# Three quarters of an output weight loaded in mid-run, in unequal shares per DMA engine: one decode step of attention and an MLP

## The chip, the cores and the metric

The kernel runs on one core of one Trainium2 chip. The core has a matrix engine (PE, with its weight loads shown as PEld), a vector engine (DVE), a scalar engine (ACT), GpSimd (POOL) and a queue engine (SP). All of them share 16 DMA engines that bring data from memory (HBM) to the on-chip buffer of 128 partitions. The metric is the device time of one execution in microseconds (us); less is better.

## The reference

One token, model width 512. Attention has 32 heads of 128 with a cache of 4096 keys and values each; beside it stands an MLP of 1376 hidden units; a gate mixes the two.

```python
g = sigmoid((x * gate_w).sum(-1))
q = (x @ wq).reshape(1, 1, 32, 128)                 # wq: 512 x 4096
p = softmax(einsum(q, k_cache) * 128 ** -0.5)       # per head: 4096 scores
a = einsum(p, v_cache).reshape(1, 1, 4096) @ wo     # wo: 4096 x 512
h = relu(x @ w1 + b1) ** 2                          # w1: 512 x 1376
b = h @ w2 + b2                                     # w2: 1376 x 512
out = g * a + (1 - g) * b
```

Everything is bf16. The caches are 32 MB each, `wq` and `wo` 4 MB each, `w1` and `w2` 1.4 MB each: 78 MB are read once for an output of 1 KB.

## The kernel before, in words

**Order of the loads.** SP issues nearly all loads into one queue, in the order of the program: four pieces of `wq` into the buffer `W`, then K and V of each head by turns, K seven heads (`LAG`) ahead of V. Each K or V is 1 MB: 128 partitions, 8 KB in each, which the 16 DMA engines share evenly. Eight buffers each (`Kt`, `Vt`); a K buffer is loaded again once DVE (`s_sd`) and PE (`s_t`) have read it, a V buffer once PE has (`s_pv`). After V 8 come the four pieces of `w1`, after V 10 the whole of `w2` (`w2a` in one load with 10 KB in each partition, `w2b` for the last 96 rows).

**Work per head.** For half of the keys DVE multiplies and sums (`ttr`, L579); for the other half PE turns them (`transposes`, L385), ACT copies them out (`evac`, L319) and PE takes the product with q (`scores`, L396). Every four heads the maxima are joined (`max_rows`, `max_cols`), ACT takes the exponentials (`exps`, L330), PE sums over the values (`pv`, L421), and every eight heads DVE divides by the denominators and the gate (`norm`, giving eight columns of `onorm` and counting `s_on`). In iteration i of the PE's loop, `transposes(i)`, `scores(i-1)` and `pv(i-7)` follow each other.

**The output weight.** `W` is free for `wo` once all of `wq` was used (`s_qps` 8, in iteration 21). `wo` is used in two parts, each laid out so that a partition holds several neighbouring rows. The first `NA` = 16 heads are the first 64 such long rows of `woa_v` (32 rows of `wo`, 32 KB each), which go to partitions 32 to 95. GpSimd loads 60 of them, in four groups, each a load of 12 partitions and one of 3. The cursor that decides at which DMA engine a load starts is reset ahead of each group, and a dummy load of 4 partitions (`dm`) goes first. Head 3 (`HX`) is left out there and is loaded by SP at the end (`wox`). The other 16 heads follow from SP in three pieces of 8, 6 and 2 rows per partition (`TS`, L251), which overwrite `W`; so SP waits for PE's last use of the first part (`s_wa`).

Because `wo` lies in long rows, the attention output must be laid out likewise. For the first part: `turn_a` (PE) turns `onA`, DVE copies it to `oA`, `spread_a` (PE) spreads it with a matrix of zeros and ones (`selA`) to `o2A`, and `out_a` makes 128 small matmuls in four quarters (iterations 28 to 31) into `acc`. For the second part `regroup` does this at the end of the run with `selB`, and `out_b` makes the matmuls, a piece at a time as it lands. The matrices are built by GpSimd in place of `w1`, once that was used (`s_h`).

**The MLP.** `mlp_h` (PE, iteration 24) makes the hidden layer, DVE squares it, and `mlp_out` (iteration 27, L451) adds its product with `w2` to `acc`.

**The end.** Behind the last data SP issues fifteen tiny loads, of 1 to 15 partitions (L254), then waits for the result and stores it. DVE adds the bias to `acc` (L655), PE turns the sum (L541), DVE copies it (L657).

Of the kernel before, what the change touches and what calls it, by code (L numbers as in the profile page):

```python
# [5 lines left out]
def bass_gated_mix__gqa_block_cached__dense_activation_squared_relu__decode_kernel(  # L6
# [47 lines left out]
    NA = 16  # L54
    HX = 3
    A0 = 32
    TB = 16
    TS = [0, 8, 14, 16]
    NW = len(TS) - 1

# [4 lines left out]
    wob_v = A_wo[NA * 128:NH * 128, :].rearrange("(p t) n -> p t n", t=TB)  # L65
# [4 lines left out]
    with ctx:  # L70
# [14 lines left out]
        wox = W[:, TB * DM:TB * DM + DM]  # L85
# [3 lines left out]
        selB = w1_sb[0:NH - NA, 0, 0:1024].rearrange("h (c p) -> h c p", c=8)  # L89
        selA = w1_sb[0:NA, 1, 0:512].rearrange("h (c p) -> h c p", c=4)  # L90
# [8 lines left out]
        onA = sb("onA", [128, NA], bf16)  # L99
# [4 lines left out]
        dm = sb("dm", [4, 4, 2, 16], bf16)  # L104
        fin4 = sb("fin4", [4, 128], bf16)
        zeros = sb("zeros", [128, 128], bf16)
        xb = sb("xb", [128, 4, 128], bf16)
        ident = sb("ident", [128, 128], bf16)
# [29 lines left out]
        O2B = pS[:, 64:64 + TB]  # L138
# [3 lines left out]
        OTA = pQ[0:NA, 0:128]  # L142
        O2A = pQ[:, 128:160]
# [16 lines left out]
        s_w2 = sem("s_w2")  # L160
        s_wo = [sem(f"s_wo{t}") for t in range(NW)]
        s_wx = sem("s_wx")
        s_wp = [sem(f"s_wp{n}") for n in range(8)]
        s_dm = [sem(f"s_dm{n}") for n in range(4)]
        s_na = sem("s_na")
        s_at = sem("s_at")
        s_ac = sem("s_ac")
        s_wa = sem("s_wa")
# [50 lines left out]
        def _(eng):  # L219
# [16 lines left out]
            for h in range(NH):  # L236
# [8 lines left out]
                if h == 10:  # L245
                    eng.dma_start(w2a[:, :, :], w2_v).then_inc(s_w2, 16)
                    eng.dma_start(w2b[:, :], B_w2[FG * 128:F, :]).then_inc(s_w2, 16)
            eng.wait_ge(s_wa, 1)
            eng.dma_start(wox, A_wo[HX * 128:HX * 128 + 128, :]).then_inc(s_wx, 16)
            for c in range(NW):  # L250
                eng.dma_start(wo_sb[:, TS[c]:TS[c + 1], :], wob_v[:, TS[c]:TS[c + 1], :])\  # L251
                   .then_inc(s_wo[c], 16)
# [10 lines left out]
        def _(eng):  # L263
# [9 lines left out]
            HI = A0 + 4 * (HX + 1)  # L273
            LO = A0 + 4 * HX
            for r in range(4):
                eng.inc_swdge_sem([], [], mode="reset_dge_cursor")
                src = B_w1[0:4, 0:32].rearrange("p (a c) -> p a c", a=2)
# [5 lines left out]
            for q in s_dm:  # L283
                eng.wait_ge(q, 16)
# [60 lines left out]
        def _(eng):  # L345
# [122 lines left out]
            def out_a(n):  # L468
# [9 lines left out]
                if n == 3:  # L478
                    mm.then_inc(s_wa, 1)
# [16 lines left out]
            def out_b(c):  # L496
# [6 lines left out]
                if c == NW - 1:  # L503
                    mm.then_inc(s_acc, 1)
# [181 lines left out]
```

## Time and profile before

| | us |
|---|---|
| median of 3 runs | 198.80 (198.79 to 198.81) |
| the profiled execution | 198.97 |
| its span, first to last instruction | 197.1 |
| busy: PE / DVE / ACT / POOL | 132.0 / 129.2 / 79.5 / 11.7 |
| bytes moved by DMA | 78.75 MB, mean 400 GB/s |
| share of the chain that ended last: DMA / DVE / SP's queue / PE | 70% / 12% / 9% / 6% |
| GpSimd's loads: first issue, last landing | 106.2, 130.6 |
| last landing of V 31 / of the three last pieces of `wo` | 188.94 / 191.76, 193.63, 194.27 |

The page of the profile cuts the span into 40 equal slices and gives for each engine the busy tenths, the clock granted to PE, the mean busy share of the 16 DMA engines and what they moved. The stretches are the same with limits of one's own choice: for each engine the busy time and the number of instructions, then the clock, the DMA share and GB/s. The chain of waits is followed back from the last instruction, at each step to what released it. The records of the landings hold a time for each step of a load's semaphore; a load counts 1 for each DMA engine that has done its share.

### The profile page before, as it was taken

The numbers are of one execution on the slowest core, as the hardware profiler recorded it, in microseconds if no ns is written. First come the engines' busy times: TensorE is split into PE (matmuls) and PEld (weight loads), VectorE is DVE, ScalarE is ACT, GpSimd is POOL, SyncE is SP. The second block draws the span as 40 slices with busy tenths as digits, with TensorE's granted clock in tenths as the row PEclk, the third lists the DMA queues.
The fourth block names the chain that finished last, engine by engine and source line by source line (L and its number), as shares of the span: only waits on it lengthen the run. The fifth ranks groups of instructions, "written<-read, shape, count | busy, mean of one in ns | idle before, by whom it ended". The sixth has DMA issues, their size and how long they took to land.

```text
span 197.1 us, 6623 instructions
## 1 busy us (share of the span) xinstructions
PE 132.0 (67%) x2455; PEld 119.0 (60%) x2461; DVE 129.2 (66%) x1144; ACT 79.5 (40%) x148; POOL 11.7 (6%) x24
## 2 busy tenths in 40 slices
PE   0138657499886867915637476756999997994444
PEld 0105637478676667715635476756999987884443
DVE  0307999999998687716835677757759987760010
ACT  2105838466463436503306333633038432623000
POOL 2000000000000000000004900000070000000000
PEclk9999966755555555555558555555555555555555
DMA  6999999999999999999999999999999999999970
GB/s 221 427 427 424 421 421 422 412 421 421 416 417 421 416 422 403 420 424 385 414 421 416 419 416 411 408 426 417 421 417 417 421 412 419 417 421 421 412 296 21
DMA packets 12262, 78.75 MB, mean 400 GB/s; under 512 B 2035, under 2 KB 2261, under 8 KB 3030
## 3 DMA queue, kind: packets, MB, share of 16 engines
q1 hardware_dynamic: 11448, 76.36, 94.0%
q0 software_dynamic: 768, 1.97, 2.6%
q8 instruction: 19, 0.31, 0.6%
q14 instruction: 13, 0.11, 0.2%
q10 hardware_dynamic: 14, 0.01, 0.0%
HBM read 78.32 MB, written 0.00 MB: 397 GB/s over the span
## 4 chain that ended last, share of the span: by engine, by line
DMA 70%; DVE 12%; SPq 9%; PE 6%; issue 1%; ACT 0%
DMA Kt<-in_A_k_cache_dram 55%; DVE Kt L579 11%; DMA W<-in_A_wo_dram 9%; SPq L232 6%; DMA W<-in_A_wq_dram 6%; PE KP L385 2%; SPq L227 2%; PE pQ L363 1%; DVE S L579 1%; SPq L221 1%; PE pX L500 1%; PE pX L475 0%; PE pQ L421 0%; PE pX L421 0%; PE pS L396 0%
## 5 line engine op out<-in xcount | busy, mean ns | idle before, releaser
L579 DVE CUSTOM_DVE_ANT_0 Kt<-Kt,qb 128x128 bf16<-128x128 bf16 x512 | 111.2, 286 | 28.2 <-DMA Kt<-in_A_k_cache_dram 28.2
L319 ACT ACTIVATE kT<-KP 128x1024 bf16<-128x1024 bf16 x64 | 61.9, 1021 | 70.8 <-PE KP L385 70.8
L385 PE MATMUL KP<-ident,Kt 128*128 128x128 bf16 x512 | 56.6, 299 | 31.7 <-DMA Kt<-in_A_k_cache_dram 31.7
L385 PEld LDWEIGHTS KP<-ident,Kt 128*128 128x128 bf16 x512 | 49.1, 139 | 34.5 <-DMA Kt<-in_A_k_cache_dram 33.1
L579 DVE DVE_READ_ACCUMULATOR2_ANT S<- 128x1 f32 x512 | 41.7, 81 | 0.0
L396 PEld LDWEIGHTS pS<-qcol,kT 128*128 128x128 bf16 x512 | 19.0, 108 | 9.2 <-DVE S L585 9.2
L396 PE MATMUL pS<-qcol,kT 128*128 128x1 bf16 x512 | 19.2, 167 | 7.9 <-DVE S L585 7.9
L363 PE MATMUL pQ<-W,xb 128*128 128x512 bf16 x26 | 12.3, 614 | 7.7 <-DMA W<-in_A_wq_dram 6.3
L421 PEld LDWEIGHTS pO<-E,Vt 128*128 128x128 bf16 x512 | 15.6, 105 | 1.2 <-issue 0.8
L421 PE MATMUL pO<-E,Vt 128*128 128x1 bf16 x512 | 16.2, 166 | 0.0
L421 PE MATMUL pQ<-E,Vt 128*128 128x1 bf16 x256 | 8.1, 165 | 7.1 <-DMA Vt<-in_A_v_cache_dram 5.4
L421 PEld LDWEIGHTS pQ<-E,Vt 128*128 128x128 bf16 x256 | 7.6, 104 | 7.4 <-issue 6.0
L311 ACT ACTIVATE qb<-pQ 128x512 bf16<-128x512 f32 x8 | 4.7, 592 | 15.1 <-PE pQ L363 15.1
L363 PEld LDWEIGHTS pQ<-W,xb 128*128 128x128 bf16 x32 | 3.6, 130 | 10.7 <-issue 10.7
L330 ACT ACTIVATE E<-S,nM 128x32 bf16<-128x32 f32 x32 | 9.9, 310 | 0.3
L278 POOL DMA_DIRECT2D dm<-in_B_w_dram x4 | 2.6, 648 | 104.3 <-PE pQ L363 104.3
L421 PEld LDWEIGHTS pX<-E,Vt 128*128 128x128 bf16 x256 | 7.8, 104 | 0.7 <-issue 0.6
L421 PE MATMUL pX<-E,Vt 128*128 128x1 bf16 x256 | 8.1, 165 | 0.0
L600 DVE RECIPROCAL rden<-pM 128x8 f32<-128x8 f32 x4 | 0.8, 203 | 10.4 <-PE pM L427 10.4
L585 DVE COPY S<-pS 128x16 f32<-128x16 f32 x32 | 5.4, 169 | 2.7 <-PE pS L396 2.7
L565 DVE CAST qcol<-pQ 128x4 bf16<-128x4 f32 x8 | 1.2, 152 | 8.4 <-PE pQ L371 8.4
L588 DVE TENSOR_REDUCE mp<-S 128x1 f32<-128x32 f32 x32 | 6.0, 186 | 1.1
(84 smaller groups left out, 79.5 us busy)
## 6 DMA issues: line engine op xcount, KB each, us to landing
Kt<-in_A_k_cache_dram SPq DMA_DIRECT2D x32, 1024.0 KB, 26.9
Vt<-in_A_v_cache_dram SPq DMA_DIRECT2D x32, 1024.0 KB, 27.8
W<-in_A_wq_dram SPq DMA_DIRECT2D x4, 1024.0 KB, 7.8
W<-in_A_wo_dram POOLq DMA_DIRECT2D x4, 384.0 KB, 12.9
w_sb<-in_B_w_dram SPq DMA_DIRECT2D x4, 344.0 KB, 22.8
w2a<-in_B_w_dram SPq DMA_DIRECT2D x1, 1280.0 KB, 18.5
W<-in_A_wo_dram SPq DMA_DIRECT2D x1, 1024.0 KB, 16.7
W<-in_A_wo_dram SPq DMA_DIRECT2D x1, 768.0 KB, 18.1
```

The lines of the kernel that those rows point to most:

```text
L227: eng.dma_start(Kt[:, h % NK, :], k_h[h, :, :]).then_inc(s_k[h % NK], 16)
L232: eng.dma_start(Vt[:, h % NV, :], v_h[h, :, :]).then_inc(s_v[h % NV], 16)
L311: eng.activation(qb[:, c * 512:(c + 1) * 512], pQ[:, :], ACT.Copy).then_inc(s_qb, 1)
L319: eng.activation(kT[:, h % 2, j * HB * 128:(j + 1) * HB * 128], KP[n % 3][:, :], ACT.Copy).then_inc(s_ev, 1)
L330: eng.activation(E[:, h % NE, :], S[:, h % NS, :], ACT.Exp, bias=nM[:, h:h + 1], scale=SCALE, accum_out=RS[:, h:h + 1]).then_inc(s_e, 1)
L363: mm = eng.matmul(pQ[:, :], xb[:, t, :], wq_sb[:, t, c * 512:(c + 1) * 512], start=(t == 0), stop=(t == 3))
L385: mm = eng.transpose(KP[n % 3][:, y * 128:(y + 1) * 128], Kt[:, h % NK, b * 128:(b + 1) * 128], ident[:, :])
L396: mm = eng.matmul(S2[:, y:y + 1], kT[:, h % 2, y * 128:(y + 1) * 128], qcol[:, h:h + 1], start=True, stop=True)
L421: mm = eng.matmul(O(h, h + 1), Vt[:, h % NV, b * 128:(b + 1) * 128], E[:, h % NE, b:b + 1], start=(b == 0), stop=(b == NB - 1))
L579: ins = eng.tensor_tensor_reduce(kb, kb, qb[:, h * 128:(h + 1) * 128], 1.0, 0.0, ALU.mult, ALU.add, S[:, h % NS, b:b + 1])
L585: eng.tensor_copy(S[:, h % NS, XB:NB], S2).then_inc(s_cp, 1)
L588: eng.tensor_reduce(mp[:, h:h + 1], S[:, h % NS, :], AX.X, ALU.max).then_inc(s_mp, 1)
```

## The change

- GpSimd now loads the rows of the first 24 heads (`NA` = 24): 96 long rows of 32 KB in 26 loads of 2, 3, 4 or 12 partitions. The table `RUNS` lists them; each entry gives a kind of place, the DMA engine at which it starts, how many engines it takes in a row (one row each), and an offset. `place` makes the partitions from it. `turns` works out how far the cursor must be moved between loads; a dummy load of so many partitions does it. There are 15 dummies; with this table no reset is needed after the one at the start of the program.
- Only the last 8 heads of `wo` remain for SP: one piece of 1 MB, 8 KB in each partition, into the K buffer 0 after K 24 was used. `W` is not loaded a second time, so the wait on `s_wa`, the piece `wox` and the detour of head 3 (`onA`) are gone.
- `w2` leaves its place after V 10 and is loaded last, as `w2b` and then `w2a` in pieces of 8 and 2 of its 10 groups.
- On PE, `turn_a` and `spread_a` go from iterations 26 and 27 to 32 and 33, `out_a` from 28-31 to 34-37; it opens the sum in `acc`. After the loop come `regroup` (16 matmuls on `selB`, where there were 8), `out_b` (32 matmuls in place of 64) and `mlp_out` in three pieces, which closes the sum.
- GpSimd builds `selA` in 26 steps, one for each load, where there was one.

```diff
-    NA = 16
-    HX = 3
-    A0 = 32
-    TB = 16
-    TS = [0, 8, 14, 16]
+    NA = 24
+    TB = 8
+    GS = [0, 8, 10]
+    INNER, OUTER, SEAM, WRAP = range(4)
+    RUNS = ([(INNER, 4, 12, r) for r in range(4)] + [(INNER, 0, 3, r) for r in range(4)]
+            + [(OUTER, 0, 3, 0), (OUTER, 3, 2, 1), (OUTER, 5, 2, 1), (SEAM, 7, 2, 1),
+               (OUTER, 9, 3, 1), (OUTER, 14, 2, 0)]
+            + [(OUTER, 4, 4, 0), (OUTER, 8, 4, 0), (WRAP, 15, 2, 1), (OUTER, 1, 2, 1)]
+            + [(SEAM, 7, 2, 2), (WRAP, 15, 2, 2), (OUTER, 1, 2, 2)]
+            + [(SEAM, 7, 2, 3), (WRAP, 15, 2, 3)])
+
+    def place(kind, e, k, r):
+        if kind == INNER:
+            return 32 + 4 * e + r, 4
+        if kind == OUTER:
+            return (4 * e if e < 8 else 64 + 4 * e) + r, 4
+        if kind == SEAM:
+            return 28 + r, 68
+        return r, 124
+
+    def turns():
+        at, out = 0, []
+        for _, e, k, _ in RUNS:
+            d = (e - at) % 16
+            out.append((False, d) if d != 1 else (True, e))
+            at = (e + k) % 16
+        return out
...
+        wob_sb = Kt[:, 0, :].rearrange("p (t n) -> p t n", t=TB)
...
 @block.sync
-                if h == 10:
-                    eng.dma_start(w2a[:, :, :], w2_v).then_inc(s_w2, 16)
-                    eng.dma_start(w2b[:, :], B_w2[FG * 128:F, :]).then_inc(s_w2, 16)
-            eng.wait_ge(s_wa, 1)
-            eng.dma_start(wox, A_wo[HX * 128:HX * 128 + 128, :]).then_inc(s_wx, 16)
-            for c in range(NW):
-                eng.dma_start(wo_sb[:, TS[c]:TS[c + 1], :], wob_v[:, TS[c]:TS[c + 1], :])\
-                   .then_inc(s_wo[c], 16)
+            eng.wait_ge(s_sd, NA + 1)
+            eng.wait_ge(s_t, 2 * (NA + 1))
+            eng.dma_start(Kt[:, 0, :], wob_v).then_inc(s_wo, 16)
+            eng.dma_start(w2b[:, :], B_w2[FG * 128:F, :]).then_inc(s_w2[0], 16)
+            for c in range(len(GS) - 1):
+                eng.dma_start(w2a[:, GS[c]:GS[c + 1], :], w2_v[:, GS[c]:GS[c + 1], :])\
+                   .then_inc(s_w2[c + 1], 16)
+            eng.wait_ge(s_sb, 1)
             for n in range(1, 16):
                 eng.dma_start(w1_sb[0:n, 3, 32 * n:32 * n + 8], B_w1[0:n, 0:8]).then_inc(s_pr[n - 1], 16)
...
 @block.gpsimd
             eng.wait_ge(s_qps, 8)
-            for r in range(4):
-                eng.inc_swdge_sem([], [], mode="reset_dge_cursor")
-                src = B_w1[0:4, 0:32].rearrange("p (a c) -> p a c", a=2)
-                eng.dma_start(dm[0:4, r, :, 0:8], src[:, :, 0:8]).then_inc(s_dm[r], 16)
-                eng.dma_start(W[HI + r:A0 + 64:4, :], woa_v[HI - A0 + r:64:4, :],
-                              max_dma_last_dim=8192).then_inc(s_wp[2 * r], 16)
-                eng.dma_start(W[A0 + r:LO:4, :], woa_v[r:LO - A0:4, :],
-                              max_dma_last_dim=8192).then_inc(s_wp[2 * r + 1], 16)
+            for n, ((back, d), run) in enumerate(zip(turns(), RUNS)):
+                if back:
+                    eng.inc_swdge_sem([], [], mode="reset_dge_cursor")
+                if d:
+                    src = B_w1[0:d, 0:32].rearrange("p (a c) -> p a c", a=2)
+                    eng.dma_start(dm[0:d, sent, :, 0:8], src[:, :, 0:8]).then_inc(s_dm[sent], 16)
+                    sent += 1
+                k = run[2]
+                p, st = place(*run)
+                eng.dma_start(W[p:p + st * (k - 1) + 1:st, :], woa_v[q:q + k, :],
+                              max_dma_last_dim=8192).then_inc(s_wp[n], 16)
+                q += k
...
             eng.wait_ge(s_h, 1)
-            eng.memset(w1_sb[0:NA, 0:2, 0:1024], 0.0).then_inc(s_sb, 1)
+            eng.memset(w1_sb[0:NA, 0:3, 0:1024], 0.0).then_inc(s_sb, 1)
             eng.wait_ge(s_sb, 1)
-            eng.affine_select(out=selA, in_=selA, compare_op=ALU.not_equal, fill=1.0,
-                              base=A0, pattern=[[1, 4], [-1, 128]], channel_multiplier=4)\
-               .then_inc(s_sb, 1)
...
+            for n, run in enumerate(RUNS):
+                k = run[2]
+                p, st = place(*run)
+                eng.wait_ge(s_sb, n + 2)
+                part = selA[:, :, p:p + st * (k - 1) + 1]
+                eng.affine_select(out=part, in_=part, compare_op=ALU.not_equal, fill=1.0, base=-st * q,
+                                  pattern=[[st, 4], [-1, st * (k - 1) + 1]], channel_multiplier=4 * st)\
+                   .then_inc(s_sb, 1)
+                q += k
...
 @block.tensor
             def turn_a():
-                eng.wait_ge(s_na, 2)
-                eng.wait_ge(s_qb, 8)
-                eng.matmul(OTA, onA[:, :], ident[:, :], start=True, stop=True).then_inc(s_at, 1)
+                eng.wait_ge(s_on, NA // HPO)
+                eng.wait_ge(s_ev, 2 * NH)
+                eng.transpose(KP[2][0:NA, 0:128], onorm[:, 0:NA], ident[:, :]).then_inc(s_at, 1)
 
             def spread_a():
                 eng.wait_ge(s_ac, 1)
-                eng.wait_ge(s_sb, 2)
+                eng.wait_ge(s_cp, NH)
+                eng.wait_ge(s_sb, 2 + len(RUNS))
...
+            def mlp_out(c):
+                eng.wait_ge(s_w2[c], 16)
+                for n in [FG] if c == 0 else range(GS[c - 1], GS[c]):
+                    M = 128 if n < FG else FR
+                    w = w2a[:, n, :] if n < FG else w2b[:, :]
+                    for j in range(4):
+                        mm = eng.matmul(acc[:, j:j + 1], w[:, j * 128:(j + 1) * 128], hs[0:M, n:n + 1],
+                                        start=False, stop=(n == FG - 1), skip_group_check=True)
+                if c == len(GS) - 1:
+                    mm.then_inc(s_acc, 1)
...
-                if i == 26:
+                if i == 32:
                     turn_a()
-                if i == 27:
-                    mlp_out()
+                if i == 33:
                     spread_a()
-                if 28 <= i < 32:
-                    out_a(i - 28)
+                if 34 <= i < 38:
+                    out_a(i - 34)
             regroup()
-            for c in range(NW):
-                out_b(c)
+            out_b()
+            eng.wait_ge(s_hs, 2)
+            for c in range(len(GS)):
+                mlp_out(c)
```

## The prediction, made before the changed kernel ran

> **What bounds the kernel now.** I read the page's slices first, then the chain of waits, then the end of the run in stretches of 1 us, then the landings of the last loads.
>
> The slices (40 of 4.9 us) show the DMA engines busy at nine tenths or more from the second slice to the 38th, at some 421 GB/s whatever the compute engines do:
>
> ```profile
> DMA  6999999999999999999999999999999999999970
> GB/s 221 427 427 424 421 421 422 412 421 421 416 417 421 416 422 403 420 424 385 414 421 416 419 416 411 408 426 417 421 417 417 421 412 419 417 421 421 412 296 21
> ```
>
> So 78.75 MB set the time, and a change that moves the same bytes can win little but where the engines stand idle: here, the end. The chain of waits ends there too:
>
> ```profile
> 175.53 18.10 DMA W<-in_A_wo_dram
> 193.63 0.05 issue
> 193.68 1.03 PE pX L500 x32
> 194.70 0.02 issue
> 194.73 0.17 DVE fin L655
> ```
>
> The last pieces of wo land, 32 matmuls follow, then what is fixed. The stretches (columns after the engines: granted clock, DMA share, GB/s) show how the transfers end:
>
> ```profile
> 186.00:188.00 2.00, 0.99 (x32) 0.94 (x32) 0.00 (x0) 0.00 (x0) 0.00 (x0) 0.50 1.02 415
> 188.00:189.00 1.00, 0.00 (x0) 0.00 (x0) 0.00 (x0) 0.00 (x0) 0.00 (x0) 0.50 0.95 369
> 189.00:190.00 1.00, 0.92 (x32) 0.94 (x32) 0.00 (x0) 0.00 (x0) 0.00 (x0) 0.50 0.69 273
> 190.00:191.00 1.00, 0.55 (x8) 0.27 (x5) 0.44 (x2) 0.00 (x0) 0.00 (x0) 0.50 0.59 240
> 191.00:192.00 1.00, 0.47 (x13) 0.43 (x13) 0.17 (x1) 0.00 (x0) 0.00 (x0) 0.50 0.54 211
> 192.00:193.00 1.00, 0.88 (x32) 0.80 (x30) 0.00 (x0) 0.00 (x0) 0.00 (x0) 0.50 0.37 103
> 193.00:194.00 1.00, 0.32 (x12) 0.33 (x13) 0.00 (x0) 0.00 (x0) 0.00 (x0) 0.50 0.09 33
> ```
>
> The share decays over 5 us: some engines are done at 189, others work until 194. The trace's landing records say which. Every load adds 1 to its semaphore for each engine, so the last piece of wo has sixteen landings, from 189.15 to 194.27, mean 191.53. The fifteen tiny loads of L254, queued behind it, name the engines: the one of n partitions has n late landings, and each next one adds a new engine. Matching the two, engines 0 to 15 end their data at 189.7, 190.7, 189.2, 193.3, 190.2, 192.7, 192.5, 189.4, 189.2, 192.3, 192.5, 192.4, 194.3, 194.1, 192.7, 189.5. Perfect levelling would bring the last landing from 194.27 to 191.53: 2.74 us are there to be had.
>
> **Part 1, the rows from GpSimd.** A row of `woa_v` is 32 KB, four packets of 8 KB at 0.312 us (the trace's packets): 1.25 us of one engine. Before, fifteen engines took 4 rows each and engine 3 none; 60 in all. After, counted from RUNS, engines 0 to 15 take 8, 7, 7, 1, 6, 6, 6, 8, 8, 6, 6, 6, 4, 4, 5, 8; 96 in all. The 36 more rows leave the evenly spread loads, so each engine loses 36/16 = 2.25 rows there. The new end of an engine is its old end + 1.25 x (new rows - old rows - 2.25): 191.9, 191.6, 190.1, 191.8, 189.9, 192.4, 192.2, 191.6, 191.4, 192.0, 192.2, 192.0, 191.5, 191.3, 191.1, 191.7. The latest is engine 5: 192.41, so -1.86 us. The bounds: -2.74 (all even), and -0.6 if an engine is out by one row (192.41 + 1.25).
>
> The issue cost lies beside the stream. POOL went from 106.20 to 113.16 for 12 loads, 0.58 us each; 41 loads (26 of rows, 15 dummies) take 24 us from about 103 (3.3 us of w2 no longer lie ahead). Before, 4 rows an engine were in 24.4 us after the first issue (last landing 130.6); 8 are in 49 us, by 152. What the smaller loads cost the stream:
>
> ```profile
> 84.00:97.00 13.00, 6.61 (x133) 6.39 (x133) 7.34 (x68) 3.88 (x4) 0.00 (x0) 0.50 1.02 406
> 112.00:131.00 19.00, 11.45 (x208) 11.10 (x209) 12.55 (x113) 7.21 (x15) 1.16 (x3) 0.50 1.02 414
> 145.00:170.00 25.00, 23.30 (x523) 22.70 (x521) 21.37 (x183) 14.02 (x30) 2.37 (x3) 0.50 1.01 418
> ```
>
> While GpSimd's 12 loads run the rate is 414 against 418 later: 4/418 x 19 = 0.18 us; 29 more would lose 0.43 at the most, 0 if those 4 GB/s are instruction fetches. I take +0.2.
>
> The Trainium skill speaks against this part twice. "DMA: Bandwidth & Descriptors", Latency and other measured facts, calls engines 7 and 15 usually slower, its guess being contention for the descriptor rings of loads issued from GpSimd; the change gives both 8 rows. The trace has them among the earliest (189.4 and 189.5) after GpSimd's loads; put by the page with the latest (194.3), their 1.75 rows more would end at 196.5, and the estimated sum would be a loss of some 2.4 us. The same page's Anatomy of one DMA gives a load from GpSimd 2.0 us of fixed cost; on the path, 29 more would add an estimated 58 us, but the row above shows the fixed part of 12 loads hidden under the stream.
>
> **Part 2, w2 goes last.** The same bytes leave slices 18 and 19 and come at the end. The stretch 84:97, where w2 landed in runs of 10 KB and 1 KB, ran at 406: (418 - 406)/418 x 13 = 0.37 us below. Now it comes as 8 KB, 2 KB and 1 KB runs. Bounds: -0.37 (the end of before, in 8, 6 and 2 KB runs, held 415), and 0 if the 10 KB stride was to blame. I take -0.15.
>
> The work behind the last landing grows. Before, the last two pieces held 24 and 8 matmuls and landed 0.64 apart; 32 took 1.01 us from 193.68. Now they hold 32 and 8, landing as far apart: 40 x 0.0315 = 1.26 us after the first. +0.25.
>
> **Part 3, the waits.** SP no longer waits for `s_wa` (4.9 us, to 174.69). That gains nothing: the pieces behind it landed 17 to 18 us after issue, queued. Its new wait for K head 24 is over 25 us before SP gets there (PE is past those transposes at 139.8; V 31 is issued near 170). The wait on `s_sb` holds back the tiny loads and the output store, and is over by 160.
>
> PE now turns and spreads at i = 32 and 33. Queued behind are pv 26 and on, and `max_cols(7)`, which the last exps wait for. `turn_a` wants the last evacuation (K 31 turned by 172.5, plus ACT's 2 x 1.02) and comes after 175: met. `spread_a` wants 28 steps of POOL:
>
> ```profile
> 143.90 1.79 POOL L286 MEMSET w_sb<- 16x2048 bf16 x1 [30.74 <-PE pX L439]
> 145.84 0.63 POOL L288 TENSOR_SCALAR_AFFINE_SELECT w_sb<-w_sb 16x512 bf16<-16x512 bf16 x1
> 146.44 1.08 POOL L291 TENSOR_SCALAR_AFFINE_SELECT w_sb<-w_sb 16x1024 bf16<-16x1024 bf16 x1
> ```
>
> From these 0.18 us + 0.88 ns an element: memset 2.7, `selB` 2.0, 26 selects over 3468 elements 7.7, and 0.15 between two: 16.4 us, done by 168 even if the dummies land at 152. It is needed near 178. `out_a` now follows pv 27 to 30, where PE idled 1.0 to 1.5 us before each pv; its 0.87 fits. If that cover were gone, pv 31 would be late, with this spare: V 31 lands 5.95 us of engine time (8 x 0.312 + 6 x 0.046 + 8 x 0.312 + 8 x 0.084) before the end, at 186.5. Before, pv 31 began at 189.08 and `out_b` at 191.86; now 8 more matmuls on `selB` (0.045 each) make this 3.2 us, and with 36 matmuls PE is ready for w2a at 190.9, 0.9 us ahead of its landing at 191.8.
>
> **Sum:** -1.86 + 0.2 - 0.15 + 0.25 = -1.56. The profiled execution took 198.97 (span 197.1), 0.17 above the median of 198.80; 198.80 - 1.56 = 197.24, rounded to **197.3 us**, own range 196.7 to 198.0.
>
> **The rivals.**
> *Better levelling* (chance 0.16): the ends meet at the mean and w2's loss goes: -2.74 - 0.37 + 0.25 = -2.86, 195.9 to 196.6. For it: the granularity of a row is finer than my spread of 2.5 us suggests. Against: engines 2 and 4 are left early by the count.
> *One engine a row late* (0.15): ends hang on instruction fetches, which fall on single engines; the trace has 32 during the run, 13 of 8 KB (0.33 us) and 19 of 16 KB (1.07 us). POOL's program grows by some 70 instructions, so one more fetch is possible. 1.25 us with 0.43 for the loads gives -0.6 to -0.1: 198.2 to 198.7.
> *Rows on the wrong engines* (0.12), slower: which engine a row lands on follows from a cursor that dummies of 13, 6, 3 and 2 rows advance; before, the cursor was reset ahead of each group and only dummies of 4 were used. Engine 3 decides: it takes 1 row because it alone would end 5 us later with 4. If a later group slips so that it gets 3 rows too many, it ends at 191.8 + 3.75 = 195.5, 1.25 after the old end: about 200.3. If all rows turn by some engines it holds 6 to 8: 198.0 to 200.5 for the last landing, 202.8 to 205.3. Against: with dummies of 4 the skipped engine did fall back from 6.2 to 3.6 us late across GpSimd's loads.
>
> **The numbers.** The forecast has 0.57. A measurement of this kernel cannot tell less than 0.2% (0.4 us) from no change. Faster: 0.57 + 0.16 + 0.06 of "one engine a row late" (its part below 198.4) = 0.79; within: 0.09; slower: 0.12. The range leaves out the slips and a little of the best case: 196.1 to 198.8.
>
> **What would show it.** The DMA share falls from 1.0 to 0.2 within some 2.5 us, not 5; the last landing near 192.4, the sixteen within 2.5 us; two groups of 32 and 8 matmuls of w2 behind it without idle time between; the rate while GpSimd loads at 412 or more; engines 7 and 15 not the last. Wrong: sixteen landings as wide as before (rows misplaced), or a PE wait for POOL in `spread_a`.

## The result, and the profile after

The changed kernel took 201.09 us (median of 6 runs, 200.66 to 201.58), the kernel before 198.76 (198.62 to 198.81): a ratio of 1.0119, 95% interval 1.0101 to 1.0137. It is slower by 2.3 us where 1.5 us less was predicted. The profiled execution took 201.05, span 199.2.

One count given ahead of the result is wrong. `RUNS` has 23 entries, not 26, and the trace shows 23 loads of rows and 15 dummies: 38 loads from GpSimd where 41 were counted, 26 more than the 12 of before, and 23 steps on `selA`. The rows and their engines (96 in all) were counted rightly.

The slices of the changed kernel (columns as before: busy tenths, or GB/s, in 40 slices, now of 4.98 us):

```profile
DVE  0307999999997687637857776765677799940001
POOL 2000000000000000000049998000000586600000
DMA  6999999999999999999999999999999999999950
GB/s 227 427 424 423 423 418 421 414 424 421 413 418 418 418 416 414 419 414 421 419 424 416 413 413 408 403 413 410 410 407 415 418 418 418 421 416 421 385 189 2
```

Three things differ from before. The rate at w2's old place has risen as foreseen (slice 19: 421, before 385), but in slices 23 to 31, while GpSimd loads, it is 403 to 415, below what lies around. DVE is at nine tenths in slices 33 to 35. And the end is no shorter: the sixteen landings of the last load lie between 190.65 and 194.44, mean 192.38 (before: 189.15, 194.27, 191.53).

The chain that ended last (start, duration, engine, line):

```profile
178.59 0.94 PE pQ L449 x32
179.53 0.68 issue
180.21 0.99 PE pX L492 x32
181.20 0.85 PE pQ L449 x32
182.06 0.85 PE pX L492 x32
182.91 0.85 PE pQ L449 x32
183.76 0.44 PE pM L455 x2
184.20 1.97 issue
186.17 0.99 PE pX L492 x32
187.16 0.85 PE pQ L449 x32
188.01 0.85 PE pX L492 x32
188.87 0.83 PE pQ L449 x31
189.69 3.04 issue
193.86 0.59 PE pS L501 x16
194.70 1.01 PE pX L510 x32
195.72 1.19 PE pX L520 x44
```

Before, this chain ended in a DMA; now its last 18 us hold only PE and what PE waits for. `pv` (L449) and `out_a` (L492) alternate, and PE stops with nothing to wait for: 0.68, 1.97 and 3.04 us, the last with one matmul of `pv` 31 to go. All of w2's matmuls come after the last landing (194.44), at 195.72. The two long stops are 127 matmuls apart (the sum of the x's between them). The 0.68 is another matter. It stands ahead of the first quarter of `out_a` in every kernel below with these 23 loads, wherever the long stops lie (0.68 to 0.77). PE has one semaphore to pass there for each load of rows. The kernel before had a long stop too, 1.68 us from 176.92, ahead of a stretch in which PE waited for V anyway:

```profile
178.60 0.22 PE L421 MATMUL pQ<-E,Vt 128*128 128x1 bf16 x3 [1.68 <-issue]
```

The DMA queues of the page name a candidate for the long stops (packets, MB, share of 16 engines):

```profile
q8 instruction: 19, 0.31, 0.6%
```

These are packets of 16 KB and 1.08 us each. The last four start at 175.7, 183.8, 190.2 and 193.9, and PE goes on 1.3 us after the second ended and 1.4 us after the third. Two counts say that they hold PE's program. There are 19 in before and in the change, 20 in each of the three kernels below with 64 or 100 matmuls more on PE, and 18 in the three with 96 matmuls less. And at each of the 19 long stops (0.9 us or more) in the kept traces PE goes on 1.2 to 1.7 us after the end of such a packet. So about 128 matmuls with their weight loads come in one packet. From go to go again it took 186.17 to 192.74, 6.6 us for 127 matmuls; V lands every 2.48 us and asks for 32 of `pv`, and `out_a` adds 32 more, so 128 in 5.0 us. With `out_a` between them PE uses its program faster than it arrived.

DVE's full slices begin with this (the timeline from 156 to 160 us, first POOL, then DVE):

```profile
156.36 2.65 POOL L307 MEMSET w_sb<- 24x3072 bf16 x1 [32.49 <-DMA xb<-in_B_w_dram]
159.16 2.01 POOL L309 TENSOR_SCALAR_AFFINE_SELECT w_sb<-w_sb 8x2048 bf16<-8x2048 bf16 x1
```

```profile
159.44 1.87 DVE L598 CUSTOM_DVE_ANT_0 Kt<-Kt,qb 128x128 bf16<-128x128 bf16 x1 [1.17 <-DMA Kt<-in_A_k_cache_dram]
```

GpSimd waited 32.5 us for its dummies, so the steps on `selA` ran from 161.3 to 173.4, and DVE's multiply of 0.29 us took 1.87 us beside the 2.01 us of the first select, and 0.42 to 0.70 beside several others. `scores(31)` then waited for DVE until 175.18; V 25, landed at 171.8, was used from 175.6.

The Trainium skill, "SBUF — State Buffer", SBUF: two separate sides, has this case: a DVE operation with two inputs in the buffer and a GpSimd operation that reads it take a shared pair of ports in turn, and the loser waits for the whole instruction. The trace agrees: the multiply ended at 161.31, the select at 161.17.

**The engines.** Ends of the data per DMA engine, found as for the prediction (engines that end close together can be exchanged by 0.2 us; the kernels of the last four columns are described below):

| engine | before | forecast | after | e1_dmlate | e5_bpad64 | e4_lvl2 | e5_lvl3 |
|---|---|---|---|---|---|---|---|
| 0 | 189.7 | 191.9 | 192.4 | 192.5 | 189.5 | 189.7 | 190.8 |
| 1 | 190.7 | 191.6 | 193.0 | 192.7 | 190.6 | 191.0 | 192.1 |
| 2 | 189.2 | 190.1 | 191.7 | 191.7 | 189.3 | 189.3 | 189.4 |
| 3 | 193.3 | 191.8 | 192.9 | 192.8 | 193.4 | 193.3 | 193.5 |
| 4 | 190.2 | 189.9 | 190.7 | 190.7 | 189.9 | 190.0 | 189.3 |
| 5 | 192.7 | 192.4 | 193.1 | 193.0 | **194.0** | **194.2** | 191.3 |
| 6 | 192.5 | 192.2 | 192.9 | 193.0 | **193.7** | 192.8 | 192.4 |
| 7 | 189.4 | 191.6 | 192.3 | 192.2 | 189.0 | 190.5 | 190.8 |
| 8 | 189.2 | 191.4 | 192.1 | 192.4 | 189.1 | 190.6 | 190.6 |
| 9 | 192.3 | 192.0 | **194.3** | 192.7 | **193.7** | 192.6 | **194.0** |
| 10 | 192.5 | 192.2 | **194.4** | 192.7 | 192.2 | 192.3 | **194.0** |
| 11 | 192.4 | 192.0 | 192.8 | 192.9 | 192.2 | 192.4 | 192.7 |
| 12 | **194.3** | 191.5 | 190.8 | 192.2 | 192.3 | 191.1 | 192.7 |
| 13 | **194.1** | 191.3 | 190.7 | 192.1 | 192.4 | 191.2 | 192.9 |
| 14 | 192.7 | 191.1 | 191.7 | 191.8 | 192.6 | **194.0** | 191.5 |
| 15 | 189.5 | 191.7 | 192.3 | 192.4 | 189.5 | 189.5 | 188.4 |

After against forecast: nearly all are 0.5 to 1.6 late, engines 9 and 10 by 2.3, and 12 and 13 are 0.7 early. The rows went where the table of RUNS says. Some 1.5 us that lay on 12 and 13 lies on 9 and 10.

The landing records show when this came about. V 30 has all its landings by 184.26. Of the sixteen of V 31, fifteen are in by 186.68 and one at 188.07. Of `w2b`'s, fifteen by 190.01 and one at 191.36; of the first piece of `w2a`, fourteen by 192.40 and two at 193.66 and 193.79. So one engine fell back by some 1.4 us during V 31 and a second during `w2a`, and packets of 16 KB start at 183.8 and 190.2. A quiet stretch of the kernel before shows the same without any rows: from load to load the landings move on by 2.48 us each, but in the loads during which the packets of 49.9, 66.5 and 84.3 came one engine moves on by 0.95 to 0.97 more (a second one by some 0.4 in two of the three, all others by 0.07 or less). The same happens near its end: the last landings of two loads that follow each other are 175.53 and 179.00, 1.0 us more than a step, while the packet of 176.1 comes, and one engine stays that late to the end. So one packet of PE's program holds up one engine.

### The profile page after: what moved, and what is told of

The parts are those of the page before. It is cut to its first block, busy times and chain, and to the rows that moved or that the text cites. A ratio compares the mean times of both kernels' runs of the same rounds, so it can differ in the third digit from the quotient of the medians.

```text
span 199.2 us, 6642 instructions
## 1 busy us (share of the span) xinstructions
PE 130.8 (66%) x2427; PEld 117.1 (59%) x2433; DVE 132.7 (67%) x1141; ACT 79.5 (40%) x148; POOL 36.2 (18%) x72
## 4 chain that ended last, share of the span: by engine, by line
DMA 60%; DVE 17%; PE 12%; SPq 6%; issue 4%; ACT 0%; DVEq 0%
DMA Kt<-in_A_k_cache_dram 54%; DVE Kt L598 15%; DMA W<-in_A_wq_dram 5%; SPq L248 4%; PE pQ L449 3%; PE KP L413 2%; PE pX L492 2%; PE pQ L391 1%; PE pO L449 1%; DVE S L598 1%; PE pS L424 1%; SPq L237 1%; PE pX L520 1%; SPq L243 1%; PE pX L510 1%
## 5 line engine op out<-in xcount | busy, mean ns | idle before, releaser
L598 DVE CUSTOM_DVE_ANT_0 Kt<-Kt,qb 128x128 bf16<-128x128 bf16 x512 | 115.4, 295 | 27.1 <-DMA Kt<-in_A_k_cache_dram 27.1
L296 POOL DMA_DIRECT2D xb<-in_B_w_dram x15 | 8.8, 585 | 100.6 <-PE pQ L391 100.6
L449 PEld LDWEIGHTS pO<-E,Vt 128*128 128x128 bf16 x512 | 15.5, 104 | 1.2 <-issue 0.8
L449 PE MATMUL pO<-E,Vt 128*128 128x1 bf16 x512 | 16.1, 165 | 0.0
L300 POOL DMA_DIRECT2D W<-in_A_wo_dram x23 | 12.8, 560 | 0.0
L449 PE MATMUL pQ<-E,Vt 128*128 128x1 bf16 x256 | 8.1, 165 | 3.0 <-issue 3.0
L318 POOL TENSOR_SCALAR_AFFINE_SELECT w_sb<-w_sb 24x36 bf16<-24x36 bf16 (+5 forms) x23 | 8.9, 388 | 3.3
L307 POOL MEMSET w_sb<- 24x3072 bf16 x1 | 2.6, 2648 | 32.5 <-DMA xb<-in_B_w_dram 32.5
L449 PEld LDWEIGHTS pX<-E,Vt 128*128 128x128 bf16 x256 | 7.8, 104 | 0.7 <-issue 0.6
L449 PE MATMUL pX<-E,Vt 128*128 128x1 bf16 x256 | 8.0, 165 | 0.0
L449 PEld LDWEIGHTS pQ<-E,Vt 128*128 128x128 bf16 x256 | 7.6, 104 | 0.1
```

The source lines that it names most:

```text
L296: eng.dma_start(dm[0:d, sent, :, 0:8], src[:, :, 0:8]).then_inc(s_dm[sent], 16)
L300: eng.dma_start(W[p:p + st * (k - 1) + 1:st, :], woa_v[q:q + k, :], max_dma_last_dim=8192).then_inc(s_wp[n], 16)
L318: eng.affine_select(out=part, in_=part, compare_op=ALU.not_equal, fill=1.0, base=-st * q, pattern=[[st, 4], [-1, st * (k - 1) + 1]], chann ...
L449: mm = eng.matmul(O(h, h + 1), Vt[:, h % NV, b * 128:(b + 1) * 128], E[:, h % NE, b:b + 1], start=(b == 0), stop=(b == NB - 1))
L598: ins = eng.tensor_tensor_reduce(kb, kb, qb[:, h * 128:(h + 1) * 128], 1.0, 0.0, ALU.mult, ALU.add, S[:, h % NS, b:b + 1])
```

## The experiments

Theories: **F**, PE lacks its program and sets the end; **G**, GpSimd's selects beside DVE make PE late; **L**, the late engines are where instruction packets fall, and move; **T**, each small load from GpSimd costs the stream. Every kernel ran beside the kernel before on its chip (medians 198.69 to 198.73 us). Nine start from the changed kernel; e3_bdup, e3_lvl, e4_lvl2, e5_lvl3 and e5_bpad64 start from the kernel before.

**e1_pad64 and e1_pad100: PE's program shifted**

```diff
+            for _ in range(64):        # 100 in e1_pad100
+                eng.matmul(pS[:, 8:9], xrow[:, 0:128], ident[0:1, 0:1], start=True, stop=True)
             for t in range(4):
                 eng.wait_ge(s_wq[t], 16)
```

> 64 small matmuls more at the start. Theory F: the stop of 3 us falls on the end of pv 30, 64 matmuls earlier, and all of the remaining work follows it: 200.8 to 201.8, and over 1.2 us above the kernel with 100. Rival G: as without the pad, 200.6 to 201.6, and equal to the kernel with 100.

> 100 small matmuls more at the start of PE's program, while PE waits for wq. Theory F (PE's instructions are fetched 16 KB, 128 matmuls with their weight loads, at a time, and a fetch beside the full DMA stream stops PE 2 to 3 us; in the changed kernel such a stop of 3.04 us falls on the last matmul of pv 31): the pad moves the stop 28 matmuls later in the code, into out_b, where PE has some slack before the last piece of w2 lands; pv 31 runs through, the time falls to 199.0 to 199.7. Rival G (GpSimd's steps on selA, which hold up DVE from 159 to 173, make PE late, and that lateness is the loss): the pad changes nothing, 200.6 to 201.6.

200.09 us, ratio 1.0066 (1.0049 to 1.0083), and 200.35 us, 1.0068 (1.0044 to 1.0093), though the profiled execution of e1_pad100 took 199.29; that gap of 1 us stays unexplained. Both kernels do more work than the change and take less time, yet neither median is in F's range, and the order of the two is not the one that F gave. The chain of e1_pad64:

```profile
185.78 0.99 PE pQ L451 x32
186.77 2.68 issue
189.45 1.01 PE pX L494 x32
190.46 0.87 PE pQ L451 x32
```

The stop now lies after `pv` 30, ahead of a quarter of `out_a`, though nothing in this part of the program was edited. In e1_pad100 it came before the last four matmuls of the third quarter of `out_a` (2.28 us at 185.67), 28 matmuls later in the code than in the change; `pv` 31 runs through, and the chain ends in a DMA again, with all of `out_a` in place:

```profile
169.43 24.32 DMA w2a<-in_B_w_dram
193.80 1.24 PE pX L522 x40
```

So the stop goes by the count of instructions, as F says; the time expected of e1_pad64 was missed, since PE had caught up with V 30 before the stop.

**e2_noouta: three of four quarters of out_a left out**

```diff
-                for t in range(8 * n, 8 * n + 8):
+                for t in range(8 * n, 8 * n + 8 if n == 0 else 8 * n):
```

> The changed kernel without the second to fourth quarter of out_a: 96 small matmuls with their weight loads less on PE in iterations 35 to 37, all loads as they were. (The rows of wo that these matmuls use are loaded and left out of the sum.) Theory F, made narrower by the first runs (the next 16 KB of PE's instructions are asked for half a piece, some 64 matmuls, ahead and take 4 to 5.5 us to come beside the full stream, so that PE cannot do more than 64 small matmuls in that time; pv and out_a together do 64 in 2.5 us): the stops of 2 and 3 us are gone or under 0.7 us before pv 31 is done, PE waits for the last piece of w2, and the end is 0.7 after the last landing: 198.2 to 199.4. Rival G (PE's lateness from DVE is the loss): it is late by the same stretch at 175 and the end moves less than 0.5: 200.3 to 201.3.

The rows of `wo` for these quarters are loaded and left out of the sum. 199.19 us, ratio 1.0012 (0.9988 to 1.0036): 1.9 below the change, where the 96 matmuls themselves are worth 2.6 us on PE and lie in its waits for V. The chain:

```profile
169.84 24.14 DMA w2a<-in_B_w_dram
194.03 1.24 PE pX L520 x40
195.50 0.28 PE KP L561
```

The long stops are gone (the 0.68 at `out_a` is still there), PE waits for V 30 (2.8 us), for V 31 and for w2a (1.5 us), and the end is a DMA's again, followed by the 40 matmuls that the prediction counted (1.24 us; worked out 1.26). F holds for 1.9 us. The last landing, 194.64, and the mean, 192.38, are near those of the change (194.44, 192.38): what is left above the forecast is in the transfers.

The ten times of this kernel run from 197.82 to 199.84, three of them under 198.2; those of the kernel before, in all its runs, from 198.53 to 199.05. No kernel was traced twice. So it was not tested whether the late engines change from one execution to the next without any edit, and this spread leaves room for it.

**e1_dmlate: GpSimd waits for its dummies last**

```diff
-            for n in range(sent):
-                eng.wait_ge(s_dm[n], 16)
             eng.wait_ge(s_h, 1)
...
+            for n in range(sent):
+                eng.wait_ge(s_dm[n], 16)
```

> GpSimd's waits for its dummy loads go to the end of its program, so that selA and selB are built from about 144 instead of 156. Rival G: DVE is held up 12 us earlier, where it has K to spare, and PE is no longer late at the end: 199.0 to 199.6. Theory F: PE is in time for pv 27 and idles before pv 31 while the next instructions come, so that the stop shrinks to 1 to 1.5 us: 199.2 to 200.0, with the stop still to be seen in pv 31. If neither holds: 200.6 to 201.6.

200.56 us, ratio 1.0091 (1.0072 to 1.0109). The selects ran from 145 to 160, and PE was waiting for V 27 at 176.8: G's lateness is gone. By the medians it is worth 0.5 us, but the intervals of this kernel and of the change overlap. Both theories had given less time (199.0 to 200.0), and F a stop of 1 to 1.5 us. The chain:

```profile
187.87 0.83 PE pQ L449 x31
188.69 3.04 issue
192.01 0.24 DVE onorm L625
```

The same matmul of `pv` 31 stops for the same 3.04 us, 1.0 us earlier. The last landing came at 192.97, at the same mean (192.35): its column in the table is the forecast's, 0.5 to 1.6 later throughout, without an engine that stands out. Engines 9 and 10 have lost their 1.5 us, and 12 and 13 are where the forecast has them, not early.

**e4_late_noouta: both together**

> The changed kernel with GpSimd's waits for its dummies at the end of its program and without three quarters of out_a (as in e2_noouta: their rows of wo are left out of the sum). Theories F and G are two costs: G alone gave 0.5, F alone 1.9. If the stops of PE are what ends the run, and DVE's delay only moves PE within them, taking both away gives no more than F alone: 198.8 to 199.4, ended by the last landing of w2. If both lie on the path: 198.3 to 198.7.

199.74 us, ratio 1.0044 (1.0027 to 1.0061), above both. The stops in pv 31 and G are gone and PE waits 1.5 us for w2a, but now engines 6 and 9 end late, as in e2_noouta, and the last landing is 194.79. The two cures don't add up: against e1_dmlate the last landing is 1.8 us later at the same mean (192.37). Against e2_noouta it is 0.15 later, and the 0.5 us between the two medians is not clear of noise (the intervals overlap).

**e2_early: out_a one iteration earlier, in e1_dmlate**

```diff
-                if 34 <= i < 38:
-                    out_a(i - 34)
+                if 33 <= i < 37:
+                    out_a(i - 33)
```

(`turn_a` and `spread_a` go with it.)

> GpSimd's waits for its dummies at the end of its program, and turn_a, spread_a and out_a one iteration earlier each (31, 32, 33 to 36), so that pv 31 has no out_a just before it. Theory F: the same matmuls have 2.5 us more to come in, the stop at the end shrinks by up to that much: 198.3 to 199.3; against the kernel that has only the waits moved (200.56) 1.2 to 2.2 less. Rival G: moving the waits was all there was to win; within 0.4 of 200.56.

200.84 us, ratio 1.0104 (1.0087 to 1.012). Missed by 1.5:

```profile
183.24 2.90 issue
186.14 0.94 PE pQ L449 x30
187.08 0.44 PE pM L455 x2
187.52 0.84 PE pX L492 x32
188.36 1.68 PE pQ L449 x63
190.04 2.52 issue
```

The time is the one that rival G gave, but not for its reason: the stops are there, 127 matmuls apart. The same number of instructions has to arrive before the same last matmul of `pv` 31; a new order among them frees nothing.

**e2_w2mid: w2 back in mid-run**

```diff
+                if h == 10:
+                    eng.dma_start(w2a[:, :, :], w2_v).then_inc(s_w2[0], 16)
+                    eng.dma_start(w2b[:, :], B_w2[FG * 128:F, :]).then_inc(s_w2[0], 16)
...
+                if i == 27:
+                    mlp_out()
```

> The rows alone: w2 back at its place after V 10 in one load, and mlp_out at iteration 27; GpSimd's loads and the K buffer for the last 8 heads stay. Theory F with T: PE has 44 matmuls less at the end, but only 2.5 us of data follow V 31, so that the chain behind V 31 (about 3.2 us and 32 matmuls) ends the run: last landing 193 to 194.5, time 199.3 to 200.5. Rival (w2's new place is what costs): back to 198.8 or less. The rate from 84 to 97 us should fall from 420 to about 406 again.

202.12 us, ratio 1.0149 (1.0113 to 1.0185): missed, slower still. Nothing of w2 is left to do at the end, and yet PE is later than in the change:

```profile
191.85 2.38 issue
194.23 0.49 PE pX L491 x13
194.72 0.87 PE pQ L448 x32
```

`pv` 31 starts at 194.72, though V 31 had landed at 190.8. The mean landing is 192.24, 0.14 earlier than in the change (the seven kernels with w2 at the end and the same 38 loads have 192.30 to 192.38): the stretch 84 to 97 runs at 407 here and 420 in the change, but 184 to 188 at 418 here and 392 there. That fits a loss that goes along with w2.

**e1_dup and e3_bdup: fifteen more small loads**, in the change and in the kernel before, of 16 partitions and 16 numbers each, to a place that nobody reads.

> 15 dummy loads of 16 partitions more from GpSimd, that move no byte that matters. Theory T (each load from GpSimd puts about 3 small packets of 9 ns on each of the 16 engines, and the 29 more of the change are the 0.8 us by which the mean of the sixteen last landings went from 191.53 to 192.38): the mean goes up by 0.4 us more, to 192.8. Rival (the mean went up for another reason, such as w2's new place or the long rows' share of one engine): it stays within 0.1 of 192.4. The time: 0 to 0.5 above the changed kernel's, since PE and not the last landing ends the run.

> The kernel before with 15 dummy loads of 16 partitions more from GpSimd. Theory T: mean and last landing 0.4 us later than in the kernel before (191.9 and 194.7), and the time too, since the landings end this kernel: 199.0 to 199.3. Rival (small packets go beside the data and cost nothing): 198.6 to 198.8.

202.01 us, ratio 1.0185 (1.0125 to 1.0245), and 199.66, 1.005 (1.0035 to 1.0065). Both are above what T gave, and the four times of e1_dup differ by 3 us (201.31 to 204.28), so T rests on the landings. The mean landing rises by 0.41 and by 0.75 us: 0.03 to 0.05 us of all sixteen engines for each small load. T holds for these dummies.

For the loads of the change there is a second count. GpSimd's queue (q0) on the pages of before and of the change (packets, MB, share of 16 engines):

```profile
q0 software_dynamic: 768, 1.97, 2.6%
q0 software_dynamic: 2320, 3.16, 4.4%
```

Of these, 240 and 384 are the rows' packets of 8 KB. The rest, 528 and 1936, are of at most 32 bytes and take 9.6 ns each on average in the trace. 1408 more of them are 0.85 us for each of the 16 engines, and the mean landing of the change rose by 0.85. Of the rise in e1_dup such packets account for 0.30 us of 0.41 and in e3_bdup for 0.32 of 0.75; the rest is open.

**e3_even_noouta: nearly even rows in e2_noouta** (27 loads in INNER and OUTER places, 7 rows for engines 0 to 2 and 4 to 6, 6 for the others, none for engine 3).

> The changed kernel without three quarters of out_a (as in e2_noouta: their rows of wo are left out of the sum), and with nearly even rows: engine 3 none, 0, 1, 2, 4, 5, 6 seven, the others six; 27 loads from GpSimd, where the change has 41. Theory L (the uneven shares were fitted to instruction fetches that now fall on other engines, so they level nothing): the last landing stays within 0.6 of that of e2_noouta (194.64), the time within 0.5 of its 199.19. Theory T: the mean of the last sixteen landings falls by 14 x 0.028 = 0.4, from 192.38 to 192.0. Rival (the shares level as computed, and it is the small packets alone that ate the gain): the last landing gets later by 1 us or more, time 200.0 to 201.

199.08 us, ratio 1.0024 (1.0006 to 1.0042); last landing 194.44 against 194.64, mean 192.10 against 192.38. Sharing the rows out by the old ends did no better than sharing them evenly: as L says. With 11 loads less than in the change (27 against 38) the mean is 0.28 earlier, where T gave 0.4 from a wrong count of 14.

**e3_lvl and e4_lvl2: the kernel before, levelled.** One row each of engines 12 and 13 is carried by 7 and 8. In e3_lvl it goes to its old place (partitions 83 and 87), in e4_lvl2 to partitions 31 and 99; the loads are the same in number and size.

```diff
-                    eng.dma_start(W[83:88:4, :], woa_v[51:56:4, :],    # e3_lvl
+                    eng.dma_start(W[31:100:68, :], woa_v[51:56:4, :],  # e4_lvl2
```

> The kernel before with one thing done alone: one row of each of engines 12 and 13, which end last, goes to engines 7 and 8; 4 more loads from GpSimd. PE's program is untouched. If the ends of before are the same in each run, the last landing falls from 194.27 to 193.4 (engine 3 is last then) and the time by as much, 197.8 to 198.3. Theory L, if fetches move about in the kernel before as well: no gain, 198.5 to 199.0.

> As e3_lvl (the kernel before; one row each of engines 12 and 13 carried by engines 7 and 8), but the two rows now go to partitions 31 and 99, which engines 7 and 8 write in the even loads, instead of 83 and 87, which engines 12 and 13 write; selA is mended for it. Theory P (in e3_lvl it was the foreign partitions: while the two rows came, from 131.5 to 134.7, packets of 8 KB took 0.35 to 0.55 us on all engines instead of 0.312, and the mean landing went up by 0.85): no such slow stretch, mean of the last landings 191.6 to 191.7, last landing near 193.4, time 197.8 to 198.4. Rival (loads of 2 rows are slow whatever they write, or the ends of before move about): 198.7 to 199.6.

199.52 us, ratio 1.0041 (1.0026 to 1.0056), and 198.84, 1.0006 (0.9997 to 1.0015): the gain was missed in both, and the second is in its rival's range. In stretches, e3_lvl first (the last three columns: granted clock, DMA share, GB/s):

```profile
131.00:132.00 1.00, 1.00 (x24) 1.00 (x23) 1.00 (x11) 1.00 (x2) 0.00 (x0) 0.50 1.10 393
132.00:133.00 1.00, 0.99 (x37) 0.90 (x34) 1.00 (x11) 0.91 (x1) 0.00 (x0) 0.50 0.97 287
133.00:134.00 1.00, 0.00 (x0) 0.00 (x0) 0.71 (x7) 0.00 (x0) 0.00 (x0) 0.50 1.08 328
134.00:135.00 1.00, 0.00 (x0) 0.00 (x0) 0.00 (x0) 0.00 (x0) 0.00 (x0) 0.50 0.99 303
```

```profile
132.00:133.00 1.00, 1.00 (x44) 1.00 (x42) 1.00 (x11) 1.00 (x2) 0.00 (x0) 0.50 1.09 443
133.00:134.00 1.00, 0.23 (x9) 0.15 (x6) 0.96 (x9) 0.16 (x1) 0.00 (x0) 0.50 0.99 401
134.00:135.00 1.00, 0.00 (x0) 0.00 (x0) 0.00 (x0) 0.00 (x0) 0.00 (x0) 0.50 1.02 410
```

With the rows in partitions that two other engines write, all engines are busy but move 328 GB/s for 4 us; (418 - 328)/418 x 4 = 0.86 us, and its mean landing is 192.38, 0.85 over before's. In e4_lvl2 the dip is gone and the mean is 191.53 again.

The Trainium skill, "SBUF — State Buffer", The DMA port swizzle, puts partitions 80 to 83 and 84 to 87 on two different ports, and the engines of a full load on a port each; two engines at one port fits the dip. That all sixteen slow down is shown here and not stated there.

Yet e4_lvl2 ends no earlier: 12 and 13 end 3.2 and 2.9 us earlier, of which a row is 1.25, and 5 and 14 are late in their stead, by 1.5 and 1.3 with no row more.

**e5_lvl3 and e5_bpad64: where do the late engines come from?** The first levels the kernel before to e4_lvl2's ends: 4, 5, 14 and 15 carry a row less, 0, 1, 7 and 8 one more, in as many loads. The second is the kernel before with the 64 matmuls of e1_pad64 on PE, and no row moved.

> The kernel before, with the last of its four groups of rows dealt out again after the engine ends of the run e4_lvl2: engines 4, 5, 14 and 15 carry a row less, engines 0, 1, 7 and 8 a row more (in partitions 3, 7, 31 and 99 of their own); the number of loads, dummies, matmuls and GpSimd instructions is that of e4_lvl2. Theory P (which engines end late is set by two instruction fetches of about 1.5 us of an engine, and they fall where the length of the programs puts them; with the lengths of e4_lvl2 on engines 5 and 14): the ends become 191.0, 192.2, 189.3, 193.3, 188.8, 192.9, 192.8, 190.5, 190.6, 192.6, 192.3, 192.4, 192.3, 192.4, 192.8, 188.2; last landing 193.3 in place of 194.2, mean still 191.5, 197.8 to 198.2 us. Rival M (they move with any edit): two other engines 1.4 us late, last landing 194.0 to 194.4, 198.6 to 199.0 us. Rival S (5 and 14 are late by themselves, no fetch): the ends as P, but so would have been those of the kernel before, where 5 and 14 ended at 192.7.

> The kernel before with 64 small matmuls early on PE, beside the load of wq, and nothing else. Theory P (the two late engines are where two instruction fetches fall): in the kernel before 12 and 13 end at 194.3 and 194.1; with PE's program half a piece longer the 1.4 us move to other engines (12 and 13 end near 192.9 and 192.7), the mean landing stays at 191.5; the last landing is 193.9 to 194.5, so 198.4 to 199.1 us, the same time with other engines late. Rival S (12 and 13 are late by themselves): the same engine ends as before. It also tells whether PE's stop at 176.9 moves in the kernel before, as it does in the changed kernel: by 64 pairs, to some 3 us earlier or later.

198.76 us, ratio 1.0004 (0.9995 to 1.0012), and 198.62, 0.9996 (0.9987 to 1.0006). In e5_bpad64 engines 12 and 13 end 2.0 and 1.7 earlier, and 5, 6 and 9 take over 1.2 to 1.4 each, at a mean of 191.45: mean, last landing (193.97) and time are as theory P says. Only PE's program had changed. The stop of PE at 176.9 moved as well (timeline of PE):

```profile
174.53 0.56 PE L398 MATMUL pS<-qcol,kT 128*128 128x1 bf16 x16
175.99 0.99 PE L423 MATMUL pQ<-E,Vt 128*128 128x1 bf16 x32 [0.90 <-issue]
```

In e5_lvl3 engines 0, 1, 3, 4 and 15 end within 0.5 us of what their rows give, 5 and 14 are 1.3 to 1.6 us below it, and 9 and 10 are 1.4 to 1.7 above. Rival M holds: the late engines are others after an edit that leaves the number of loads as it was. No version tried is faster than the kernel before; e4_lvl2, e5_lvl3 and e5_bpad64 equal it.

## Why the prediction was wrong

The forecast was 197.3; the changed kernel is 3.8 us above. Three terms make that up, with 0.1 to spare: the levelling, 1.4 (last landing 194.44 against 192.97 in e1_dmlate); the landings as a whole, 0.6 (192.97 against 192.41 worked out); PE's end, 1.9 (e2_noouta). The first two come from one trace of each kernel.

- *Part 1, the ends of the engines (-1.86).* The counting of rows was right: in e1_dmlate all engines end 0.5 to 1.6 us behind the list, and the last landing is 192.97, 0.56 over the 192.41 worked out. The failed step was to take the old ends as fixed properties of the engines. Some 1.5 us of something else lay on 12 and 13, and it left them when nothing but PE's program was changed (e5_bpad64); in the change two engines fall back while packets of PE's program come (the landings of V 31 and `w2a`), and 9 and 10 are the ones that end late, while 12 and 13 had been given only four rows, where others carry up to eight. The prediction's rival "one engine a row late" had the cause (fetches fall on single engines), but from a longer GpSimd program, not from the same fetches falling elsewhere. The -1.86 needed the packets to stay where they were; it came out as +0.17. Of eight traced kernels with these shares and 38 loads, the last landing is 192.97 in one, and 194.40 to 194.79 in seven: that one is luck of the place.
- *Part 1, the small loads (+0.2, bound 0.43).* Mis-sized: the mean landing rose by 0.85 us, as much as 1408 more small packets take. There were 26 loads more and not 29. The bound was read from the rate over 19 us, 414 against 418 GB/s; the mean of the sixteen landings and a count of the packets show what a rate over a stretch blurs. The rate while GpSimd loads, 403 to 415, was the sign against it that the prediction had named (412 or more).
- *Part 2, w2 (-0.15) and its tail (+0.25).* The loss in 84 to 97 went away (406 to 420 GB/s), but reappeared at the end; taken together about +0.1 by the mean landing of e2_w2mid. The tail was right: 1.24 us where DMA sets the end.
- *Part 3, out_a in PE's idle time ("its 0.87 fits").* The step that cost most. It compared busy time with idle time on PE and left out what brings PE its instructions. The stop of 1.68 us in before's trace from 176.92 was there to be read, hidden by a wait for V. 127 matmuls took 6.6 us to come, and are asked for in 5.0. So PE was not ready 0.9 us ahead of w2a (190.9, with a landing at 191.8): it came to w2 at 195.72, 1.9 us after the first piece of w2a had landed (193.79), and e2_noouta won those 1.9 us.
- *Part 3, GpSimd's selects.* 23 and not 26, done at 173.4 and not by 168: the dummies took until 156.4 where 152 was allowed, and the steps on `selA` 12.1 us, gaps included; `spread_a` never waited for them, so that step held. What it didn't count is their effect on DVE (+3.5 us of busy time over the run). It cost some 0.5 us by the medians, not clear of noise, and nothing was won by its cure where PE's stops were gone (e4_late_noouta).
- *The rivals.* "Rows on the wrong engines" fell: the cursor did as the table says. The sign given for it, landings as wide as before, came all the same. "Better levelling" fell with the forecast. The time that the wrong-engines rival gave (200.3) is near what was measured, for another reason. Engines 7 and 15, with 8 rows each, ended at 192.3, in the middle of the sixteen: the Trainium skill's warning about them ("DMA: Bandwidth & Descriptors", Latency and other measured facts) didn't show.

Still open: by what rule a packet falls on an engine (PE's program alone doesn't set it: the change and e1_dmlate share one); whether it changes from one execution to the next; why e1_pad100 took 1 us more in the timed rounds than in its profile; and whether a layout levelled to the places where they do fall would gain. In the two attempts (e4_lvl2, e5_lvl3) they fell elsewhere.

## What to carry to other kernels

Before levelling DMA engines by their ends, find out whether the late ones are late by their own data: lengthen one engine's program by some idle instructions, and trace one kernel twice (which was not done here); if other engines are late, there is nothing stable to level. When small matmuls are moved into idle time beside a saturated stream, count instructions as well as microseconds; a stop that no wait explains, at even distances in instructions, is the sign. A term for many small loads is measured by doubling them, or by counting their packets, not by the rate of a stretch.

## What the runs showed of the hardware

- PE's program arrives in packets of 16 KB and 1.08 us: 19 of them in before and in the change, 20 with 64 or 100 matmuls more, 18 with 96 less. Beside a full stream PE's long stops lie 127 matmuls apart, and 6.3 to 7.0 us from go to go.
- Such a packet holds up one DMA engine, by 0.95 to 0.97 us in a quiet stretch of the kernel before. The last ones make two or three engines end 1.2 to 1.7 us late, and which ones differs between the kernels traced (12 and 13; 9 and 10; 5 and 14; 5, 6 and 9); the mean of the landings stays (191.53, 191.45, 191.53, 191.66 in four forms of the kernel before).
- Two rows of 32 KB written by engines 7 and 8 to partitions 83 and 87 slowed all sixteen engines to 328 GB/s for 4 us; to partitions 31 and 99 they did not.
- 15 more loads of 16 partitions of 32 bytes each from GpSimd cost all engines 0.03 to 0.05 us for each load. 26 more loads in the change brought 1408 more packets of 9.6 ns, 0.85 us of each engine.
